# Attention inputs loaded tile by tile at separate points of the turn, row stores behind normalising, most zero stores later

## The chip, the cores and the metric

The kernel runs on one core of a Trainium2 chip. The metric is the device time of one execution in microseconds (us). TensorE has two clock levels, 1.2 and 2.4 GHz; the profile gives the granted clock as a share of the higher one.

## The reference: what is computed

Chunked local attention over q, k, v (8 batches, 8 heads, 576 positions, 64 wide, chunks of 64), then a noisy top-2 mixture of eight experts over the 4608 resulting rows of 512:

```python
scores = scale * np.matmul(q_c, k_c.transpose(0, 1, 2, 4, 3))
scores = scores - np.max(scores, axis=-1, keepdims=True)
attn = np.exp(scores)
attn = attn / (np.sum(attn, axis=-1, keepdims=True) + 1e-09)
out = np.matmul(attn, v_c)
...
noisy_logits = logits + noise_scale * noise
top2 = np.argpartition(-noisy_logits, 2, axis=1)[:, :2]
...
h = np.maximum(x[mask] @ w1[e], 0.0)
out[mask] += top2_w[mask, k, None] * (h @ w2[e])
```

## The kernel before, in words

**Tiling.** The 4608 rows are 36 tiles of 128. Attention runs in turns: `attend(it)` (line 679) is called with `it` from 0 to 35 (line 721), once more after that loop, and four more times from a hook inside the first expert block. A turn works on several tiles at once: scores of tile `it` on TensorE, their maximum and difference on VectorE and their exponential on ScalarE, the transpose of the probabilities of tile `it-1`, the product with v (`pv`) and the normalising (`norm_a`, `norm_b`, `norm_c`) of tile `it-2`, and the transpose of the finished rows (`x_trans`) of tile `it-3`. Every fourth turn adds the gate's matrix products, and `step_route` feeds in the routing of groups of tiles piece by piece.

**Order.** The schedule is written out by hand: each engine runs its instructions in the order of the code, and SP, which issues the plain DMAs, does so too. A DMA that must wait for an engine holds up all DMAs that stand behind it in SP's order. q, k and v are loaded by pairs of tiles: `load_q`, `load_k` (512 KB each) and `load_v` (520 KB). The loads of a pair stand at the start of every second turn and those of v at the end of every second turn. A tile's finished rows go to the buffer `xbuf` in HBM from within `x_trans` (line 464), one turn after `norm_c` wrote them.

**Around it.** The first expert's weights are loaded during attention: four loads of w1 in turns 12, 15, 18 and 21 (512 KB each), and four of w2 in turns 29, 31, 33 and 35. The output must be zeroed before experts add to it: 37 stores of 256 KB, of which `zero_out(1)` puts one into each turn from 20 to 35, and `hook_tail` (line 740) the other 21 into the first expert block (`layer1(0)`). `route` builds lists of rows; with them GpSimd gathers the rows of an expert block from `xbuf` (line 240), and later adds the results into the output (line 272). After attention the expert blocks follow one another on TensorE (`three`, line 305).

Of the kernel before, what the change touches and what calls it, by code (L numbers as in the profile page):

```python
# [8 lines left out]
FT = mybir.dt.float32  # L9
# [10 lines left out]
P = 128  # L20
NTOK = 4608
NT = NTOK // P
# [38 lines left out]
def kernel(ctx, tc, qT, kT, vh, wgn, noise, w1, w2, out, caps=CAPS):  # L61
    nc = tc.nc
# [4 lines left out]
    xbuf = dram.tile([NROWS, DM], FT, name="xbuf")  # L67
# [33 lines left out]
    for c in sorted(set(caps[1:])):  # L101
        n = caps.index(c, 1)
# [11 lines left out]
    stage = ctx.enter_context(tc.tile_pool(name="stage", bufs=4))  # L114
    W = {}
    staged = {}
# [3 lines left out]
    def w_load(e, which, c):  # L120
        st = stage.tile([P, 1024], FT, name="st")
        staged[e, which, c] = st
        if which == 1:
            nc.sync.dma_start(st, w1v[ds(place[e], 1), c].rearrange("o j r f -> (o j) r f") if e else w1[e, c * P:(c + 1) * P, :])
        else:
            nc.sync.dma_start(st.rearrange("p (f n) -> p f n", f=2),
                              w2[ds(place[e], 1) if e else slice(0, 1), 2 * c * P:(2 * c + 2) * P, :]
                              .rearrange("o (f p) n -> p (o f) n", f=2))
# [11 lines left out]
    PS = ctx.enter_context(tc.tile_pool(name="psum", bufs=1, space=PSUM)).tile([P, 8, 512], FT, name="PS")  # L140
# [221 lines left out]

    pa = ExitStack()
    pk = ExitStack()
    vs = pa.enter_context(tc.tile_pool(name="vs", bufs=4, side="right"))
    work = pa.enter_context(tc.tile_pool(name="work", bufs=3, side="right"))
    gx = pa.enter_context(tc.tile_pool(name="gx", bufs=2, side="right"))
    loads = pk.enter_context(tc.tile_pool(name="loads", bufs=4))
    qp, kb, vb = {}, {}, {}

    def load_q(j):
        qp[j] = loads.tile([P, 2, 4, P], FT, name="qp")
        if j:
            nc.sync.dma_start(qp[j], qT[:, 2 * j:2 * j + 2])

    def load_k(j):
        kb[j] = loads.tile([P, 2, 4, P], FT, name="kb")
        if j:
            nc.sync.dma_start(kb[j], kT[:, 2 * j:2 * j + 2])
        else:  # L380
            for t in range(2):
                nc.sync.dma_start(qp[0][:, t], qT[:, t])
                nc.sync.dma_start(kb[0][:, t], kT[:, t])

    def load_v(j):
        vb[j] = vs.tile([P, 2, 2, 4, 65], FT, name="vb")
        nc.sync.dma_start(vb[j], vh[:, 2 * j:2 * j + 2])

    nc.scalar.preload_act_table_set("natural_log_exp_and_others")
    for j in range(2):  # L390
        load_q(j)
        load_k(j)
    load_v(0)
    load_q(2)
    load_k(2)
    load_v(1)
    wg = consts.tile([P, ND, 32], FT, name="wg")
    nc.sync.dma_start(wg, wgn)
    nz = consts.tile([P, NT, NE], FT, name="nz")
# [1 line left out]

    zero = consts.tile([P, DM], FT, name="zero")
    nc.gpsimd.memset(zero, 0.0)
    nc.sync.dma_start(xbuf[0:P, :], zero)
    load_v(2)

    PR, PT, XS, XT, RC = {}, {}, {}, {}, {}

# [2 lines left out]
    HC = [(h, c) for h in range(2) for c in range(2)]  # L411

    def scores(t):
        q, k = qp[t // 2], kb[t // 2]
        for hp in range(4):
            for h, c in HC:
                r, s = slice(h * 64, h * 64 + 64), slice(c * 64, c * 64 + 64)
                o = 256 * (t % 2) + 64 * hp
                nc.tensor.matmul(PS[s, h, o:o + 64], q[r, t % 2, hp, s], k[r, t % 2, hp, s], start=True, stop=True)

    def soft_max(t):
        mx = work.tile([P, 2, 4], FT, name="mx", bufs=2)
        nc.vector.tensor_reduce(mx, sco(t), AX.X, OP.max)
        return mx

    def soft_sub(t, mx):
        PR[t] = work.tile([P, 512], FT, name="pr", bufs=2)
        nc.vector.tensor_tensor(by_head(PR[t]), sco(t), mx[:, :, :, None].to_broadcast([P, 2, 4, 64]), OP.subtract)
# [4 lines left out]
    def p_trans(t):  # L433
        for hp in range(4):
            nc.tensor.transpose(PS[:, 2, hp * P:(hp + 1) * P], PR[t][:, hp * P:(hp + 1) * P], ident)
        PT[t] = work.tile([P, 4, P], FT, name="pts", bufs=2)
        nc.scalar.activation(PT[t].rearrange("p a b -> p (a b)"), PS[:, 2, :], AF.Copy)
# [1 line left out]
    pvb = PS[:, 3:5, 0:260].rearrange("p b (g n) -> p b g n", n=65)  # L439

    def pv(t):
        v = vb[t // 2]
        for hp in range(4):
            for h, c in HC:
                r, s = slice(h * 64, h * 64 + 64), slice(c * 64, c * 64 + 64)
                nc.tensor.matmul(PS[s, 3 + h, hp * 65:hp * 65 + 65], PT[t][r, hp, s], v[r, t % 2, c, hp, :],  # L446
                                 start=True, stop=True)

    def norm_a(t):
        RC[t] = work.tile([P, 2, 4, 1], FT, name="rc", bufs=2)  # L450
        nc.scalar.activation(RC[t], pvb[:, :, :, 64:65], AF.Identity, bias=eps)

    def norm_b(t):
        nc.vector.reciprocal(RC[t], RC[t])

    def norm_c(t):
        XS[t] = work.tile([P, DM], FT, name="xs", bufs=5)
        nc.vector.tensor_tensor(by_head(XS[t]), pvb[:, :, :, 0:64], RC[t].to_broadcast([P, 2, 4, 64]), OP.mult)  # L458

    def x_trans(t):  # L460
        g, r = divmod(t, 4)
        if r == 0:
            XT[g] = gx.tile([P, ND, 4, P], FT, name="xt", bufs=1)
        nc.sync.dma_start(xbuf[(t + 1) * P:(t + 2) * P, :], XS[t])
        for d in range(ND):
            nc.tensor.transpose(PS[:, 5, d * P:(d + 1) * P], XS[t][:, d * P:(d + 1) * P], ident)  # L466
        nc.scalar.activation(XT[g][:, :, r, :], PS[:, 5, :].rearrange("p (d n) -> p d n", d=ND), AF.Copy)
# [3 lines left out]
    def gate_mm(g):  # L471
        for d in range(ND):
            nc.tensor.matmul(PS[32 * d:32 * d + 32, 6, :], wg[:, d, :], XT[g][:, d], start=True, stop=True)  # L473
        LS[g] = gx.tile([P, 4, P], FT, name="ls", bufs=1)
        nc.scalar.activation(LS[g].rearrange("p a b -> p (a b)"), PS[:, 6, :], AF.Copy)
# [3 lines left out]
    def gate_sum(g):  # L479
        q = grp_of[4 * g]  # L480
        t0, n = groups[q]
        if 4 * g == t0:
            Z[q] = gate.tile([P, n, 2, NE], FT, name=f"gz{q % 2}")
        for r in range(4):
            nc.tensor.matmul(PS[:, 6, 16 * r:16 * r + 16], LS[g][:, r, :], sel, start=True, stop=True)  # L485
        nc.scalar.activation(Z[q][:, 4 * g - t0:4 * g - t0 + 4].rearrange("p g a e -> p (g a e)"), PS[:, 6, 0:64], AF.Copy)
# [167 lines left out]
    def step_route(n):  # L654
        for _ in range(n):
            while routing:
                try:
                    next(routing[0])
                    break
                except StopIteration:  # L660
                    routing.pop(0)
# [11 lines left out]
    def zero_out(n):  # L673
        for _ in range(n):
            if zeros:
                r = zeros.pop(0)
                nc.sync.dma_start(out[r * P:(r + 1) * P, :], zero)

    def attend(it):
        STEPS = 2 if it < 33 else 3  # L680
        if it % 2 == 0 and it >= 2 and it // 2 + 2 < NT // 2:
            load_q(it // 2 + 2)
            load_k(it // 2 + 2)
        if it in (12, 15, 18, 21):
            w_load(0, 1, (it - 12) // 3)
        if it < NT:
            scores(it)
        if 0 <= it - 2 < NT:
            pv(it - 2)
            norm_a(it - 2)  # L690
        if 0 <= it - 1 < NT:
            p_trans(it - 1)
        if 0 <= it - 3 < NT:
            x_trans(it - 3)
        if it - 5 >= 0 and (it - 5) % 4 == 3:
            gate_sum((it - 5) // 4)
            if grp_of[it - 5] != grp_of.get(it - 4):
                routing.append(route(grp_of[it - 5]))
        if it - 4 >= 0 and (it - 4) % 4 == 3:
            gate_mm((it - 4) // 4)  # L700
        if it < NT:
            mx = soft_max(it)
            step_route(STEPS)
            soft_sub(it, mx)
            soft_exp(it)
        if 0 <= it - 2 < NT:
            norm_b(it - 2)
            norm_c(it - 2)
            if 0 <= it - (NT - 3) < 3:
                x_tile(0, it - (NT - 3), at=(6, 6, 5)[it - (NT - 3)])  # L710
            step_route(4 * STEPS)
        if it % 2 == 1 and it >= 3 and (it - 3) // 2 + 3 < NT // 2:
            load_v((it - 3) // 2 + 3)
        if it in (18, 19, 21, 22, 24, 25, 27, 28):
            w_split(0, 1, *wq.pop(0), eng=nc.gpsimd)
        if 20 <= it < NT:
            zero_out(1)
        if it in (29, 31, 33, 35):
            w_load(0, 2, (it - 29) // 2)

    for it in range(NT):
        attend(it)
# [118 lines left out]
    with tc.If(n_over > 0):  # L841
# [44 lines left out]
        with tc.For_i(0, n_over) as i:  # L886
# [19 lines left out]
            for f in range(NF):  # L906
                hp_ = PS[:, 1 + f % 2, 0:P]
                for d in range(ND):
                    nc.tensor.matmul(hp_, wa[:, d, f * P:(f + 1) * P], xt[:, d, :],
                                     start=(d == 0), stop=(d == ND - 1))  # L910
# [43 lines left out]
```

## Time and profile before

| | us |
|---|---|
| median of three runs | 1015.32 (1014.34 to 1018.19) |
| the profiled execution, its own time | 1017.64 |
| its span, first to last instruction | 1015.7 |
| TensorE busy in the span | 963.1 |
| VectorE / ScalarE / GpSimd busy | 459.0 / 310.4 / 479.8 |

The profiled execution had a mean granted clock of 0.985. A turn is the time from one tile's first score product (line 419) to the next tile's. Each engine's idle time carries the name of what ended it; "issue" means that the engine waited for nothing that the profile shows. The DMA queue q1 carries what SP issues, q8 and q14 carry instructions for the engines, q0 what GpSimd issues.

### The profile page before, as it was taken

How to read it: one execution, taken by the hardware profiler on the slowest of the kernel's cores; microseconds unless marked ns; L12 is line 12 of the kernel's file. 1: busy time of each engine (PE TensorE's matmuls, PEld its weight loads, DVE VectorE, ACT ScalarE, POOL GpSimd, SP SyncE). 2: the span in 40 equal slices, each digit the busy share in tenths (PEclk: the TensorE clock that was granted, in tenths of full speed). 3: DMA queues.
4: the chain of work that ended last, by engine and by line, in shares of the span. 5: the costliest groups of instructions: out<-in, count | busy, mean ns of one | idle time of the engine just before them, and what ended most of it. 6: DMA issues, size and time to landing. Idle time of an engine off the chain costs nothing.

```text
span 1015.7 us, 18418 instructions
## 1 busy us (share of the span) xinstructions
PE 963.1 (95%) x7353; PEld 859.0 (85%) x7353; DVE 459.0 (45%) x1001; ACT 310.4 (31%) x689; POOL 479.8 (47%) x619
## 2 busy tenths in 40 slices
PE   5878889999999999999999999999999999999994
PEld 4666768898888889988998999899988998899983
DVE  5577865653534343435333533453345334434311
ACT  3567765321323132213221322132223222223100
POOL 1023725335677568356734674467346725611111
PEclk9899998999999999999999999999999999999998
DMA  9979966333431543244324342444344334411212
GB/s 347 336 242 369 329 245 238 63 106 60 128 62 43 130 132 65 41 119 134 66 42 111 115 91 50 100 124 93 62 108 124 63 69 100 129 26 26 32 24 41
DMA packets 52233, 121.53 MB, mean 120 GB/s; under 512 B 8320, under 2 KB 9216, under 8 KB 52144
## 3 DMA queue, kind: packets, MB, share of 16 engines
q1 hardware_dynamic: 31984, 81.64, 22.2%
q0 software_dynamic: 20160, 38.69, 20.6%
q8 instruction: 58, 0.95, 0.4%
q14 instruction: 31, 0.25, 0.1%
HBM read 81.56 MB, written 38.73 MB: 118 GB/s over the span
## 4 chain that ended last, share of the span: by engine, by line
PE 82%; DVE 1%; issue 0%; ACT 0%; POOL 0%
PE PS L305 79%; PE PS L334 1%; PE PS L599 1%; PE PS L288 0%; DVE xl L296 0%; ACT xh L295 0%; POOL gohp L607 0%; PE PS L466 0%; DVE o L343 0%; PE PS L222 0%; DVE gmi L527 0%; PE PS L446 0%; PE PS L473 0%; PE PS L485 0%; DVE xs L458 0%
## 5 line engine op out<-in xcount | busy, mean ns | idle before, releaser
L260 POOL DMA_INDIRECT xg<-xbuf,piece x257 | 261.1, 1016 | 78.8 <-issue 71.0
L305 PE MATMUL PS<-xh,w1h 128*128 128x384 f32 (+2 forms) x768 | 263.2, 343 | 0.1
L305 PE MATMUL PS<-xl,w1h 128*128 128x384 f32 (+2 forms) x768 | 260.8, 340 | 0.3 <-DVE xl L296 0.3
L305 PE MATMUL PS<-xh,w1l 128*128 128x384 f32 (+2 forms) x768 | 260.6, 339 | 0.0
L305 PE MATMUL PS<-w2h,hh 128*128 128x512 f32 x584 | 228.8, 392 | 0.3 <-issue 0.3
L305 PE MATMUL PS<-w2l,hh 128*128 128x512 f32 x584 | 227.7, 390 | 0.2 <-issue 0.2
L305 PE MATMUL PS<-w2h,hl 128*128 128x512 f32 x584 | 227.7, 390 | 0.0
L272 POOL DMA_INDIRECT out<-o,lid x73 | 117.0, 1602 | 230.4 <-DVE o L343 208.8
L324 DVE SCALAR_TENSOR_TENSOR hl<-PS,hh 128x384 fp32r<-128x384 f32 (+1 forms) x192 | 107.0, 559 | 227.5 <-ACT hh L323 163.9
L323 ACT ACTIVATE hh<-PS 128x384 fp32r<-128x384 f32 (+1 forms) x192 | 94.1, 491 | 364.1 <-PE PS L305 313.1
L305 PEld LDWEIGHTS PS<-xh,w1h 128*128 128x128 f32 x768 | 144.6, 188 | 3.5 <-issue 0.8
L305 PEld LDWEIGHTS PS<-xl,w1h 128*128 128x128 f32 x768 | 144.6, 188 | 2.3 <-DVE xl L296 0.5
L305 PEld LDWEIGHTS PS<-xh,w1l 128*128 128x128 f32 x768 | 144.5, 188 | 1.0
L343 DVE TENSOR_SCALAR o<-PS,lwt 128x512 f32<-128x512 f32 x73 | 54.5, 749 | 190.7 <-PE PS L305 153.1
L305 PEld LDWEIGHTS PS<-w2h,hh 128*128 128x128 f32 x584 | 109.2, 187 | 23.9 <-issue 1.6
L305 PEld LDWEIGHTS PS<-w2h,hl 128*128 128x128 f32 x584 | 109.2, 187 | 23.5
L305 PEld LDWEIGHTS PS<-w2l,hh 128*128 128x128 f32 x584 | 109.2, 187 | 23.2 <-issue 0.9
L607 POOL TENSOR_SCALAR gohp<-row_p,gpf 128x128 f32<-128x128 f32 x36 | 26.6, 782 | 111.3 <-DVE gpf L591 101.1
L295 ACT ACTIVATE xh<-y 128x512 fp32r<-128x512 f32 x67 | 41.2, 615 | 109.1 <-DVE y L292 77.7
L296 DVE TENSOR_TENSOR xl<-y,xh 128x512 fp32r<-128x512 f32 x67 | 45.1, 673 | 48.0 <-ACT xh L295 31.0
L292 DVE STREAM_TRANSPOSE y<-xg 128x512 f32<-128x512 f32 x67 | 45.6, 680 | 2.3 <-DMA xg<-xbuf,piece 2.3
L138 DVE TENSOR_TENSOR w2l<-st,w2h 128x512 fp32r<-128x512 f32 x64 | 44.9, 702 | 0.0
(139 smaller groups left out, 792.9 us busy)
## 6 DMA issues: line engine op xcount, KB each, us to landing
st<-in_w SPq DMA_DIRECT2D x64, 512.0 KB
out<-zero SPq DMA_DIRECT2D x37, 256.0 KB
vb<-in_vh SPq DMA_DIRECT2D x18, 520.0 KB
xbuf<-xs SPq DMA_DIRECT2D x36, 256.0 KB
qp<-in_qT SPq DMA_DIRECT2D x17, 512.0 KB
kb<-in_kT SPq DMA_DIRECT2D x17, 512.0 KB
xg<-xbuf,piece POOLq DMA_INDIRECT x257
out<-o,lid POOLq DMA_INDIRECT x73
```

Source lines behind the costliest of these rows:

```text
L138: (eng or nc.vector).tensor_sub(lo[:, s], st[:, s], hi[:, s].bitcast(FT))
L260: nc.gpsimd.indirect_dma_start(out=XG[e, j][:, t * P:(t + 1) * P], out_offset=None, in_=xpieces, in_offset=bass.IndirectOffsetOnAxis(ap=pi ...
L272: s = nc.gpsimd.indirect_dma_start(out=to, out_offset=bass.IndirectOffsetOnAxis(ap=rows, axis=0), in_=o, in_offset=None, compute_op=OP.add)
L292: nc.vector.transpose(y[:, 0:4 * r], x[:, 0:4 * r])
L295: nc.scalar.activation(oh, src, AF.Copy)
L296: nc.vector.tensor_sub(ol, src, oh.bitcast(FT))
L305: nc.tensor.matmul(p, a, b, start=first and n == 0, stop=last and n == 2)
L323: nc.scalar.activation(hh[:, 0:m], p, AF.Relu)
L324: nc.vector.scalar_tensor_tensor(hl[:, 0:m], p, 0.0, hh[:, 0:m].bitcast(FT), op0=OP.max, op1=OP.subtract)
L334: nc.tensor.matmul(p[32 * q:32 * q + 32, 0:P], HF[0][:, f, 32 * t:32 * t + 32], w[:, q * P:(q + 1) * P], start=(f == 0), stop=(f == NF - 1))
L343: nc.vector.tensor_scalar(o[0:r], p[0:r], weights_of(i, j)[0:r], None, op0=OP.mult)
L607: nc.gpsimd.tensor_scalar(ohp[:, 0], row_p, pf[:, 0, 0, r:r + 1], None, op0=OP.is_equal)
```

## The change

- q, k and v have one buffer per tile in place of one per pair. `load_q` and `load_k` of tile `it+4` stand behind `scores(it)`, and `load_v` of tile `it+4` behind `pv(it-2)`; each moves 256 KB (v 260 KB). There are four buffers for q and k (four pairs before), and six for v (four pairs before).
- Before the first turn, four tiles of q, k and v are loaded (before: three pairs).
- The store of a tile's rows to `xbuf` moves from `x_trans` into `norm_c`, one turn earlier in SP's order.
- The first expert's weights come in halves of 256 KB, one a turn: w1 in turns 11 to 18, w2 in turns 28 to 35.
- Of the 37 zero stores, six stay in the last three turns of attention (two a turn), and 31 go to `hook_tail`. The zero store to the head of `xbuf` moves from before the first turn to turn 8.

```diff
-    vs = pa.enter_context(tc.tile_pool(name="vs", bufs=4, side="right"))
+    vs = pa.enter_context(tc.tile_pool(name="vs", bufs=6, side="right"))
...
+    def load_q(t):
+        qp[t] = loads.tile([P, 4, P], FT, name="qp")
+        nc.sync.dma_start(qp[t], qT[:, t])
...
+    def load_v(t):
+        vb[t] = vs.tile([P, 2, 4, 65], FT, name="vb")
+        nc.sync.dma_start(vb[t], vh[:, t])
...
-    for j in range(2):
-        load_q(j)
-        load_k(j)
-    load_v(0)
-    load_q(2)
-    load_k(2)
-    load_v(1)
+    for t in range(4):
+        load_q(t)
+        load_k(t)
+        if t:
+            load_v(t - 1)
...
-    nc.sync.dma_start(xbuf[0:P, :], zero)
-    load_v(2)
+    load_v(3)
...
     def norm_c(t):
...
+        nc.sync.dma_start(xbuf[(t + 1) * P:(t + 2) * P, :], XS[t])
...
     def x_trans(t):
...
-        nc.sync.dma_start(xbuf[(t + 1) * P:(t + 2) * P, :], XS[t])
...
+    def half_load(which, n):
+        c, h = divmod(n, 2)
+        if h == 0:
+            staged[0, which, c] = stage.tile([P, 1024], FT, name="st")
+        src = w1[0, c * P:(c + 1) * P, h * 512:h * 512 + 512] if which == 1 else w2[0, n * P:(n + 1) * P, :]
+        nc.sync.dma_start(staged[0, which, c][:, h * 512:h * 512 + 512], src)
+
     def attend(it):
         STEPS = 2 if it < 33 else 3
-        if it % 2 == 0 and it >= 2 and it // 2 + 2 < NT // 2:
-            load_q(it // 2 + 2)
-            load_k(it // 2 + 2)
-        if it in (12, 15, 18, 21):
-            w_load(0, 1, (it - 12) // 3)
         if it < NT:
             scores(it)
+        if it + 4 < NT:
+            load_q(it + 4)
+            load_k(it + 4)
         if 0 <= it - 2 < NT:
             pv(it - 2)
+        if it + 4 < NT:
+            load_v(it + 4)
+        if 0 <= it - 2 < NT:
             norm_a(it - 2)
...
-        if it % 2 == 1 and it >= 3 and (it - 3) // 2 + 3 < NT // 2:
-            load_v((it - 3) // 2 + 3)
...
-        if 20 <= it < NT:
-            zero_out(1)
-        if it in (29, 31, 33, 35):
-            w_load(0, 2, (it - 29) // 2)
+        if 11 <= it < 19:
+            half_load(1, it - 11)
+        if NT - 8 <= it < NT:
+            half_load(2, it - NT + 8)
+        if it == 8:
+            nc.sync.dma_start(xbuf[0:P, :], zero)
+        if NT - 3 <= it < NT:
+            zero_out(2)
```

## Rows read from the trace of the kernel before

**Rows 1.** Busy time by stretch: length, PE, PEld, DVE, ACT, POOL, clock, DMA share, GB/s.
```profile
20.00:54.00 34.00, 26.70 (x631) 21.81 (x633) 18.33 (x35) 17.74 (x38) 0.00 (x0) 0.85 0.87 319
...
205.00:1015.70 810.70, 794.54 (x4255) 717.92 (x4253) 322.73 (x547) 194.68 (x407) 414.78 (x527) 0.99 0.35 82
```

**Rows 2.** Waits of PE in 17:54: total us, times, longest us.
```profile
PE PS L466 <- issue: 2.2, 1, 2.2
```

**Rows 3.** Timeline of PE: start us, us, instruction, idle before it.
```profile
17.59 1.02 PE L419 MATMUL PS<-kb,qp 64*64 64x64 f32 x31
...
20.18 0.69 PE L419 MATMUL PS<-kb,qp 64*64 64x64 f32 x32
...
24.43 0.37 PE L435 MATMUL PS<-ident,pr 128*128 128x128 f32 x1 [2.08 <-issue]
...
25.59 1.13 PE L419 MATMUL PS<-kb,qp 64*64 64x64 f32 x32
...
29.41 1.13 PE L419 MATMUL PS<-kb,qp 64*64 64x64 f32 x32
...
51.34 0.56 PE L446 MATMUL PS<-vb,pts 64*64 64x65 f32 x18 [1.33 <-issue]
```

**Rows 4.** Busy time by stretch again, columns as in Rows 1.
```profile
18.10:24.42 6.32, 3.93 (x127) 3.31 (x127) 4.28 (x8) 2.96 (x7) 0.00 (x0) 0.94 1.03 407
24.42:37.68 13.26, 12.13 (x254) 9.97 (x253) 6.55 (x12) 8.15 (x17) 0.00 (x0) 0.77 0.91 338
...
25.00:30.00 5.00, 5.00 (x96) 4.22 (x98) 2.18 (x4) 2.96 (x6) 0.00 (x0) 0.50 0.92 362
45.00:50.00 5.00, 5.00 (x126) 3.75 (x118) 2.33 (x5) 2.49 (x6) 0.00 (x0) 0.74 1.02 380
```

**Rows 5.** DMA queues (packets, MB, share) in 21.9:23.1, then 51.4:52.4, then 52.4:53.8.
```profile
q8 instruction: 1, 0.02, 5.5%
...
q1 hardware_dynamic: 11, 0.02, 6.3%
...
q8 instruction: 1, 0.02, 5.4%
```

**Rows 6.** Timeline of SP's queue, first issue and that at 23.96.
```profile
0.72 0.41 SPq L382 DMA_DIRECT2D qp<-in_qT  x1
...
23.96 5.51 SPq L464 DMA_DIRECT2D xbuf<-xs  x2
```

**Rows 7.** What the DMA engines moved in 0:24.4.
```profile
DMA packets 3022, 8.40 MB, mean 344 GB/s; under 512 B 327, under 2 KB 583, under 8 KB 3020
```

**Rows 8.** Waits of PE in 108:150.
```profile
PE PS L446 <- issue: 1.2, 3, 0.4
PE PS L466 <- issue: 1.1, 1, 1.1
```

**Rows 9.** Waits of PE in 0:17, and line 419's waiting instructions (ns).
```profile
PE PS L419 <- DMA kb<-in_kT: 7.2, 2, 4.2
...
L419 PEldq EVENT_SEMAPHORE  x19: 51/51/51, 4.1 to 138.5; - x19
```

**Rows 10.** DMA in 3:5 (loads of 2 KB packets), and SP's zero stores after attention.
```profile
DMA packets 291, 0.54 MB, mean 270 GB/s; under 512 B 27, under 2 KB 27, under 8 KB 291
...
159.50 14.31 SPq L677 DMA_DIRECT2D out<-zero  x21
```

**Rows 11.** Timelines of POOL and PE after attention.
```profile
181.48 1.05 POOL L240 DMA_INDIRECT xg<-xbuf,lid  x1 [4.38 <-DVE lid L211]
...
189.98 1.65 POOL L272 DMA_INDIRECT out<-o,lid  x1 [4.84 <-DVE run L552]
...
187.08 0.60 PE L288 MATMUL PS<-ident,xg 128*128 128x128 f32 x4
```

**Rows 12.** Timeline of PE: scores of tiles 11 and 19.
```profile
44.68 1.13 PE L419 MATMUL PS<-kb,qp 64*64 64x64 f32 x32
...
77.04 0.69 PE L419 MATMUL PS<-kb,qp 64*64 64x64 f32 x32
```

More of the change, by code (lines that the diff above doesn't have):

```diff
@@ L369, with load_k @@
     qp, kb, vb = {}, {}, {}
[L371 to L387, printed above, removed]
-    nc.scalar.preload_act_table_set("natural_log_exp_and_others")
-    for j in range(2):
-        load_q(j)
-        load_k(j)
-    load_v(0)
-    load_q(2)
-    load_k(2)
-    load_v(1)
+    def load_q(t):
+        qp[t] = loads.tile([P, 4, P], FT, name="qp")
+        nc.sync.dma_start(qp[t], qT[:, t])
+    def load_k(t):
+        kb[t] = loads.tile([P, 4, P], FT, name="kb")
+        nc.sync.dma_start(kb[t], kT[:, t])
+    def load_v(t):
+        vb[t] = vs.tile([P, 2, 4, 65], FT, name="vb")
+        nc.sync.dma_start(vb[t], vh[:, t])
+    nc.scalar.preload_act_table_set("natural_log_exp_and_others")
+    for t in range(4):
[3 more added lines that the diff above has]
+            load_v(t - 1)
     wg = consts.tile([P, ND, 32], FT, name="wg")
@@ L413, in scores @@
     def scores(t):
-        q, k = qp[t // 2], kb[t // 2]
+        q, k = qp[t], kb[t]
         for hp in range(4):
@@ L418, in scores @@
                 o = 256 * (t % 2) + 64 * hp
-                nc.tensor.matmul(PS[s, h, o:o + 64], q[r, t % 2, hp, s], k[r, t % 2, hp, s], start=True, stop=True)
+                nc.tensor.matmul(PS[s, h, o:o + 64], q[r, hp, s], k[r, hp, s], start=True, stop=True)
     def soft_max(t):
@@ L441, in pv @@
     def pv(t):
-        v = vb[t // 2]
+        v = vb[t]
         for hp in range(4):
@@ L445, in pv @@
                 r, s = slice(h * 64, h * 64 + 64), slice(c * 64, c * 64 + 64)
-                nc.tensor.matmul(PS[s, 3 + h, hp * 65:hp * 65 + 65], PT[t][r, hp, s], v[r, t % 2, c, hp, :],
+                nc.tensor.matmul(PS[s, 3 + h, hp * 65:hp * 65 + 65], PT[t][r, hp, s], v[r, c, hp, :],
                                  start=True, stop=True)
```

## The prediction

> **What bounds the kernel now.** I read the busy time by stretch first. After 205 us TensorE (PE) is busy 794.5 of 810.7 us [rows 1]: the expert blocks are bound by PE, and the change does not touch their work. So whatever attention gains or loses moves the end by as much. Between 20 and 54 us it is otherwise: PE is busy 26.7 of 34 us, and at a mean clock of 0.85 [rows 1]. Next I read PE's waits in that stretch, and what stands out are not the inputs. No wait for a load of q, k or v is among them; the long ones are "issue": 2.2 us [rows 2], 1.33 us, and 2.08 us in the middle of a group of four transposes, whose operands were all there [rows 3]. Their sum is 5.6 us.
>
> What does PE wait for in mid-group? The counts tell. From 18.10 us, where PE last paused, to 24.42, the end of the 2.08 us stall, PE and its weight loads ran 127 and 127 instructions; from there to the stall that ends at 37.68 they ran 254 and 253 [rows 4]. The pauses stand 254 or so instructions apart, or twice that. And inside each there is a packet of 0.02 MB on the instruction queue: one lies in 21.9 to 23.1 us, and PE goes on at 24.43 [rows 3, 5]. So PE is out of instructions, and waits for its next block.
>
> How late is a block? I take it that it is asked for when the block before it is begun. The one just named was then asked for at 18.10 and started at about 21.9: 3.8 us of waiting while SP's queue was full. Its transfer (5.5% of 16 engines over 1.2 us, 1.06 us) and the 1.4 us up to 24.43 make the rest of the 6.3 us. One with an idle queue shows the floor: after the 1.33 us stall, which ends at 51.34 [rows 3], the share of SP's queue is 6.3%, and the next block starts just behind 52.4 [rows 5], 1.1 us after it was asked for. A block then costs 1.1 + 1 + 1.4 = 3.5 us. A plain turn takes 2.59 us (17.59 to 20.18) [rows 3] and has 144 instructions by the code (32 + 32 + 4 + 4 products, each with its weight load), so 254 last 4.6 us. A block is hidden if it waits up to about 2 us; at 3.8 it is not. So this stretch is bound by instruction blocks that stand behind bursts of data.
>
> **The change part by part.** The profiled execution took 1017.64 us, 2.3 above the median of 1015.32; I sum against the profile and carry the difference over to the median.
>
> **Loads by tile, gated by the turn.** How full is the queue in either kernel? By 24.4 us SP had issued, from 0.72 to 23.96 [rows 6], 26 DMAs: four of 256 KB for the first pair, ten of 512 KB for q and k, five of 520 KB for v, four stores and one zero store of 256 KB, and 208 KB of gate and noise: 10.5 MB. Moved were 8.40 MB [rows 7]. So 2.1 MB stood in line. With the changed code and PE at the same point (scores of tile 5 and pv of tile 3 done, rows of tile 3 written) SP may have issued q, k and v of ten tiles, four stores and the 208 KB: 9.2 MB. That leaves 0.8 MB. As 2.1 MB mean a wait of some 3.8 us, 0.8 MB mean about 1.4 us: under the 2 us that a turn hides. It stays so if the DMAs keep up: four transfers a turn at 0.68 us each (21 zero stores in 14.31 us [rows 10]) are 2.7 us, against the 3.1 us that a turn takes on average here once the gate's products are in it (estimate: 2.6 us, and about 1 us more in every second turn).
>
> What there is to win: the 5.6 us of stalls, and the slow clock behind them. After the 2.1 us stall the granted clock is 0.50 (1.2 GHz) from 25 to 30 us, and after the 2.2 us one it is 0.74 on average from 45 to 50 [rows 4]. The turn from 25.59 to 29.41 takes 3.82 us in place of 2.59 [rows 3], so 1.2 us lost; in 45 to 50 about half the time is slow, so some 0.65. Together 7.45 us. I take 80%, since the queue starts full and the first block may still come late: **-6.0** (bounds 0 and -7.5).
>
> The same loss is there later: PE's "issue" waits in 108 to 150 us are 1.2 and 1.1 us [rows 8], while a zero store stood in every turn. Without it 2.3 us can go; 80% is **-1.8** (bounds 0 and -2.3).
>
> **Start.** PE waited 7.2 us for k in two waits [rows 9], 4.2 for the first tile, which the change leaves alone, and 3.0 for the second, whose two transfers are the third and fourth in either order. What stands behind them is smaller. I take **-0.5** (bounds -3.0 and +1.3, the latter if a packet lags again).
>
> **More waits.** Line 419 has 19 waiting instructions of 51 ns [rows 9]; single tiles want some 18 more, and v's may want as many: **+0.9** (bounds 0 and +1.8). What is queued behind them is PE's own turn. On SP each load now waits for PE (q and k for the scores that free their buffer, v for pv), and behind it wait that turn's store, its half of weights and the next loads. Nobody needs them within three turns (7.8 us at 2.6), so that costs nothing as long as a load lands within that time.
>
> **Row stores and weights.** The store waits for `norm_c` of its own turn where it waited for the last turn's; readers are gathers many turns later. The w1 halves come in turns 11 to 18, and their first splitting is in turn 18, so nothing waits. Nothing for these.
>
> **Zero stores.** Ten more go behind attention: 10 x 0.68 = 6.8 us of queue [rows 10]. Cover: the first addition into the output is issued at 189.98, waiting for VectorE, not for zeros [rows 11]; 31 stores from 159.5 would end at about 180.6. PE there runs long products, and a block of instructions lasts far longer. The gathers issued from 181.48 are needed at 187.08 [rows 11]; with attention shorter by 7 us both move, and the last zeros with them. Six zeros and w2's halves crowd turns 33 to 35: a block could come late once: **+0.5** (bounds 0 and +2).
>
> Sum: -6.0 - 1.8 - 0.5 + 0.9 + 0.5 = -6.9, thus 1010.7 for an execution like the profiled one, and **1008.4** beside the median.
>
> The DMA page of the Trainium skill ("DMA: Bandwidth & Descriptors", section "Rules for kernel authors") speaks against small transfers: full bandwidth wants at least 1 MiB in each DMA. In the row above 256 KB stores run back to back at 385 GB/s, which does not bear it out; by the page alone the loads would get slower, and the sum would be that of the second rival.
>
> **Rivals.** *The blocks don't hang on the queue (no change).* The block's request can't be seen; if blocks start late by a rule of their own, and not because they stand behind data, the stalls stay, and only start, waits and the end count: -0.5 + 0.9 + 0.5 = +0.9, so 1016. For it: I inferred the request. Against it: with an idle queue the block started 1.1 us after the stall's end, with a full one 3.8 us. I give it 0.25. The Trainium skill ("Runtime: NRT & Kernel Launch", section "Instruction fetch mechanics") has a rule of that kind: blocks of 16 KiB (256 instructions) are fetched ahead of time and crossing into the next is mostly hidden, and PE's memory holds 2048 of them; by it there would be no such stall to win back. The trace agrees with 256 and 16 KiB, and not with "hidden".
>
> *Loads by 2 KB pieces are slow (slower).* From 3 to 5 us only loads of 256 KB ran, at 270 GB/s [rows 10], which is 0.97 us each. If that held throughout, turns 11 to 18 would need 3 x 0.97 + 0.68 + 0.97 for the half of weights = 4.56 us of DMA; they take (77.04 - 44.68)/8 = 4.05 now [rows 12]. 0.5 x 8 = 4.1 us, the stalls stay as the queue stays full, and the last three turns with six zeros add some 3, waits 0.9: +8, so 1023. It decides where a load takes over 0.84 us (4 x 0.84 + 0.68 = 4.05). Against it: those 2 us are the start, when the engines were not all busy yet. I give it 0.08.
>
> *Half.* Blocks get earlier, but the first three stalls of the start stay, as the queue is full from the initial loads whatever the order: about -3, so 1012. I give it 0.07.
>
> **How the numbers follow.** Forecast 0.60, with a range of its own from 1002 (all bounds good) to 1012. 0.5% is 5.1 us, about what a measurement of this kernel can tell from no change. Of the forecast's 0.60, 0.55 lie below 1010.2 and 0.05 above. So faster 0.55; same 0.05 + 0.25 + 0.07 = 0.37; slower 0.08. The range of 8 in 10 is 1002 to 1016.5: below lie 0.04, above the slow rival and some of the no-change case, together about 0.15.
>
> **What would show it.** Right: PE's "issue" waits before 54 us under 2 us in sum where 5.6 stand now; clock near 1.00 from 25 to 30 and from 45 to 50; the scores of tile 19, at 77.04 now [rows 12], at about 70.5; no wait of PE for loads after tile 3; the 31 zero stores done before the first addition into the output. Wrong: stalls that stay 254 instructions apart with the same lengths though the queue is emptier; waits of line 419 for k or q; turns of over 4 us at 11 to 18 with a DMA share of 1.

## The result, and the profile after

The changed kernel takes 1010.02 us in the median (1008.16 to 1010.53), the kernel before, run beside it, 1017.53 us (1014.34 to 1018.56). The ratio is 0.9917, with a 95% interval of 0.9896 to 0.9938: about 7.5 us faster, where -6.9 was forecast. The two profiled executions, 1017.64 and 1010.38 us, are 7.3 us apart, and their spans, 1015.7 and 1008.6 us, 7.1 us.

Busy time by stretch of the kernel after (columns as in [rows 1]):

```profile
20.00:54.00 34.00, 25.26 (x686) 20.36 (x685) 22.37 (x68) 20.50 (x46) 0.00 (x0) 1.00 1.01 371
54.00:150.00 96.00, 79.72 (x1778) 66.08 (x1778) 72.07 (x244) 65.94 (x167) 39.66 (x51) 0.95 0.81 274
205.00:1008.60 803.60, 786.76 (x4217) 710.39 (x4215) 319.32 (x541) 191.21 (x400) 412.43 (x524) 1.00 0.35 81
```

The first line answers to the first of [rows 1]. In the same 34 us PE ran 686 products where it had run 631, in less busy time, as the clock was 1.00 and no longer 0.85. The DMA engines did not get any emptier: their share went from 0.87 to 1.01, and 319 GB/s became 371. The second line holds something that nothing had forecast: the clock is 0.95 there. In the profile of before on which the prediction rests it is 1.00, and in another profile of before, taken later, 0.95 too (the same stretch in these two):

```profile
54.00:150.00 96.00, 78.30 (x1887) 64.32 (x1879) 73.72 (x244) 68.84 (x175) 39.80 (x51) 1.00 0.88 312
54.00:150.00 96.00, 81.01 (x1853) 66.86 (x1849) 73.01 (x243) 67.73 (x172) 39.60 (x51) 0.95 0.87 306
```

So a slow clock there is not shown to come from the change. The last line of the three has nearly the work of before (4217 products against 4255, the window is not cut at the same instruction), so the expert blocks are as they were.

PE's waits between 17 and 54 us, all of them "issue" that the view lists (columns as in [rows 2]):

```profile
PE PS L426 <- issue: 2.4, 1, 2.4
...
PE PS L437 <- issue: 1.5, 2, 0.8
...
PE PS L457 <- issue: 0.6, 1, 0.6
```

That is 4.5 us. The same view of before has 6.0 us (the 5.6 us of the three large ones and 0.4 us). So PE still runs out of instructions. The long pause stands in turn 5 as it did before [rows 3], again in the middle of a group of four transposes (PE's timeline, columns as in [rows 3]):

```profile
18.06 0.69 PE L410 MATMUL PS<-kb,qp 64*64 64x64 f32 x32
...
19.45 0.44 PE L426 MATMUL PS<-ident,pr 128*128 128x128 f32 x2
22.31 0.38 PE L426 MATMUL PS<-ident,pr 128*128 128x128 f32 x2 [2.43 <-issue]
...
23.06 0.69 PE L410 MATMUL PS<-kb,qp 64*64 64x64 f32 x32
23.57 0.65 PE L437 MATMUL PS<-vb,pts 64*64 64x65 f32 x32
...
25.46 0.69 PE L410 MATMUL PS<-kb,qp 64*64 64x64 f32 x32
```

The difference is in what follows. The turn behind the pause takes 2.40 us (23.06 to 25.46), where before it took 3.82 us [rows 3] at a clock of 0.50 [rows 4].

Where did the gain arise? The starts of the score products, tile by tile, give a ledger (us, from PE's timelines). The first two columns are the profiles spoken of so far; "again" is a second profile of each kernel, from executions of 1014.99 and 1014.33 us, reported below:

| start of | before | after | gain so far | before, again | after, again | gain so far |
|---|---|---|---|---|---|---|
| tile 1 | 8.34 | 7.16 | 1.2 | 7.25 | 7.06 | 0.2 |
| tile 5 | 20.18 | 18.06 | 2.1 | 19.58 | 17.64 | 1.9 |
| tile 13 | 53.65 | 46.37 | 7.3 | 53.62 | 47.58 | 6.0 |
| tile 23 | 92.70 | 85.37 | 7.3 | 92.66 | 86.59 | 6.1 |
| tile 24 | 98.47 | 92.03 | 6.4 | 99.93 | 93.44 | 6.5 |
| tile 26 | 105.06 | 98.63 | 6.4 | 106.52 | 100.03 | 6.5 |
| tile 27 | 108.88 | 103.90 | 5.0 | 111.82 | 105.38 | 6.4 |
| tile 29 | 117.40 | 112.40 | 5.0 | 120.32 | 113.87 | 6.5 |
| tile 30 | 121.91 | 115.60 | 6.3 | 123.52 | 117.08 | 6.4 |
| tile 35 | 144.41 | 138.13 | 6.3 | 145.98 | 141.63 | 4.4 |
| first expert block | 151.84 | 145.55 | 6.3 | 153.41 | 149.06 | 4.4 |
| end of the span | 1015.7 | 1008.6 | 7.1 | 1013.2 | 1012.4 | 0.8 |

Before tile 13 already 7.3 us are won, and 6.0 us in the second pair: this part is in both. In the first pair the turns of tiles 23 and 26 give back 0.9 and 1.5 us, and the turn of tile 29 wins 1.3 us; in the second pair none of the three is there, but the turn of tile 31 gives back 2.1 us. The last 0.8 us of the first pair lie behind the start of the expert block, and I did not trace them to a line. In the second pair 3.6 us are lost there, and the products of line 334, spoken of below, take 4.1 us longer in that profile of after.

The two turns of after that give back in the first pair run at a slow clock (busy time by stretch, columns as in [rows 1]):

```profile
84.00:88.00 4.00, 2.34 (x67) 2.11 (x68) 3.88 (x28) 1.42 (x3) 1.27 (x1) 0.76 0.74 255
88.00:92.00 4.00, 2.73 (x24) 1.57 (x22) 2.48 (x8) 2.01 (x5) 0.00 (x0) 0.81 0.71 245
100.00:104.00 4.00, 4.00 (x43) 3.71 (x39) 3.87 (x7) 3.65 (x11) 4.00 (x6) 0.61 0.93 311
```

and the first of them starts behind a pause that has nothing to do with DMAs. PE waits there for VectorE's softmax (PE's timeline):

```profile
85.37 0.69 PE L410 MATMUL PS<-kb,qp 64*64 64x64 f32 x32 [2.18 <-DVE pr L419]
86.35 1.15 PE L437 MATMUL PS<-vb,pts 64*64 64x65 f32 x32 [0.29 <-DVE gm L514]
```

At full clock 32 products of line 437 take 0.65 us (at 23.57 above), here 1.15. Before has the same pause in the same place:

```profile
92.70 0.69 PE L419 MATMUL PS<-kb,qp 64*64 64x64 f32 x32 [2.22 <-DVE pr L428]
```

In this profile its clock stays at 1.00 behind the pause (92 to 96 us), and the turns of tiles 23 and 26 take 5.77 and 3.82 us. In the second profile of before they take 7.27 and 5.30 us, as slow as in after (6.66 and 5.27).

### The profile page after: what moved, and what is told of

Read it like the earlier page. It is cut to its first block, busy times and chain, and to the rows that moved or that the text cites. A ratio compares the mean times of both kernels' runs of the same rounds, so it can differ in the third digit from the quotient of the medians.

```text
span 1008.6 us, 18542 instructions
## 1 busy us (share of the span) xinstructions
PE 959.2 (95%) x7353; PEld 856.3 (85%) x7353; DVE 458.0 (45%) x1001; ACT 309.6 (31%) x689; POOL 479.6 (48%) x619
## 4 chain that ended last, share of the span: by engine, by line
PE 82%; DVE 1%; issue 1%; ACT 0%; another core or an unknown queue 0%; POOL 0%; DVEq 0%; ACTq 0%
PE PS L305 79%; PE PS L334 1%; PE PS L590 1%; ACT xh L295 0%; PE PS L288 0%; DVE xl L296 0%; POOL gohp L598 0%; PE PS L457 0%; DVE o L343 0%; PE PS L222 0%; ACT hh L323 0%; DVE gmi L518 0%; PE PS L437 0%; PE PS L464 0%
```

## Experiments

The prediction's theory was: the loads are the source (**A** in the texts on record), because they are released turn by turn and so fewer bytes stand ahead of an instruction block. Against it stood that the blocks have a rule of their own and do not hang on the data. The profile after raised two more questions, as the DMA engines were as full as before and the time was still won: is it the **size** of the transfers (**C**) or the **point** at which they are released (**D**)? A ratio below is to the kernel before, beside it on the same chip, with its 95% interval. The median of before was between 1010.9 and 1017.6 us in these comparisons, so ratios are to be compared, not times.

### One part alone

**Only the loads tile by tile**, in the kernel before; row stores, weights and zeros stay.

```diff
+    def load_q(t):
+        qp[t] = loads.tile([P, 4, P], FT, name="qp")
+        nc.sync.dma_start(qp[t], qT[:, t])
...
+        if it + 4 < NT:
+            load_q(it + 4)
+            load_k(it + 4)
```

> The kernel before with the tile-by-tile loads alone; weights, row stores and zero stores stay where they were. Theory A (the loads in small pieces, gated by the turn, let PE's instruction blocks come earlier and spare the slow clock): most of the gain is here, -5 to -7 us, with tile 13's scores near 46.5 us (53.65 before, 46.37 with the whole change) and the later stall of 1.1 us near turn 30 still there. Rival B (the gain comes from the zero stores and weights that were moved): within 1.5 us of before.

Measured: 0.9948 (0.9927 to 0.9969), 1011.20 us against 1017.63 us, so 5 us or so of the whole gain. From the scores of tile 5 to those of tile 13 its profile has 27.19 us, against 33.47 in before and 28.31 in after. The loads carry most of the gain. Tile 13 starts at 45.59 us, even before the 46.5 that was expected; the later stall near turn 30 is not there, though the zero stores stand where they stood (the turn of tile 29 takes 3.20 us, and 4.51 in before).

**Only the zero stores later**, in the kernel before.

```diff
-        if 20 <= it < NT:
-            zero_out(1)
+        if it == 8:
+            nc.sync.dma_start(xbuf[0:P, :], zero)
+        if NT - 3 <= it < NT:
+            zero_out(2)
```

> The kernel before with the zero stores alone moved. The first 75 us are then as before. Theory A: only the later block waits go (2.3 us before, 1.3 of it regained at turn 30 with the whole change), so -1 to -2 us. Rival B: -5 or more.

Measured: 0.9988 (0.9965 to 1.0011). If it brings anything, it is about 1 us, which these runs do not tell from nothing. Tile 13 starts at 50.98 us in its profile (53.65 and 53.62 in the two of before), where no change was expected before 75 us.

**All but the loads.** The changed kernel, with q, k and v loaded by whole pairs at the old places.

```diff
-        if it + 4 < NT:
-            load_q(it + 4)
-            load_k(it + 4)
...
+        if it % 2 == 0 and it >= 2 and it // 2 + 2 < NT // 2:
+            load_q(it // 2 + 2)
+            load_k(it // 2 + 2)
```

> The changed kernel with q, k and v loaded as before (whole pairs of 512 and 520 KB at their old places); weights in halves, row stores, zero stores and the head's zero store are the changed ones. Theory C (the size of the loads makes most of the gain): -0.5 to -2.5 us against before. Rival (the parts overlap, and the rest would give the gain alone too): -5 or more.

Measured: 0.9987 (0.9966 to 1.0007). Row stores, weights in halves and zero stores together are worth some 1.3 us if anything, which is not told from nothing.

### Size or place

**Only the size.** The kernel before, each transfer of a pair issued as two of 256 KB, at the old places and into the old buffers.

```diff
-            nc.sync.dma_start(qp[j], qT[:, 2 * j:2 * j + 2])
+            for t in range(2):
+                nc.sync.dma_start(qp[j][:, t], qT[:, 2 * j + t])
```

> The kernel before with each load of a pair issued as two DMAs of half the size at the same place in SP's order; buffers and gates are those of pairs. Theory C (what counts is how many bytes SP can have outstanding; smaller DMAs bound it): more than half of the gain of the small loads, -3 to -5 us, the blocks' waits before 54 us under 4 us. Theory D (what counts is that loads are released by the turn they follow): no change, within 1.5 us.

Measured: 0.9943 (0.9917 to 0.9970). This is as much as the loads tile by tile gave, without any new place. PE's "issue" waits in 17 to 54 us of its profile are still 4.9 us, more than was expected, and tile 5 to 13 takes 31.98 us; the profiled execution (1013.46 us) is above this kernel's median of 1012.15 us.

**The size without the place, with all the rest.** The changed kernel, loads by pairs at the old places, each as two of 256 KB. It differs from "all but the loads" above in the size alone, and from the changed kernel in place and buffers of the loads alone.

```diff
-        if it + 4 < NT:
-            load_q(it + 4)
-            load_k(it + 4)
...
+            for t in range(2):
+                nc.sync.dma_start(qp[j][:, t], qT[:, 2 * j + t])
```

> The changed kernel, but q, k and v are loaded by pairs of tiles at the places of the kernel before, each pair as two DMAs of 256 KB. Theory C (smaller DMAs are what helps; where they are released does not matter): within 1.5 us of the changed kernel, so -6.5 to -9. Theory D (release by tile at separate points helps by itself): at least 2 us slower than the changed kernel, so -6 or less.

Measured: 0.9948 (0.9929 to 0.9967); the changed kernel once more, on the same chip:

> The changed kernel once more, for a second profile and for times beside the runs below. Expected: -7 to -9 us. If the stalls before 54 us and the spells of slow clock are set by the program they stand at the same turns as in the first profile (stall in turn 5 of about 2.4 us, slow clock in turns 23 and 26); if they are chance they stand elsewhere while the time is the same.

gave 0.9936 (0.9913 to 0.9959). The two are not told apart: the place brings nothing that these runs can show. The size does: 0.9948 against 0.9987, each to before on its own chip. Their profiles say where: tile 5 starts at 18.44 us with halves and 19.81 us with whole pairs (1.4 us); tile 5 to 13 takes 26.69 against 28.76 us (2.1 us); tile 13 to 35 takes 90.82 against 93.22 us (2.4 us). That is 5.8 of the 5.9 us between the spans (1007.9 and 1013.8 us). But 1.7 of the last 2.4 us are the turn of tile 23 (5.23 against 6.89 us), which differs by 1.5 us between the two profiles of before as well.

The second profile of the changed kernel answers what was asked of it: the pause stands in turn 5 again (2.0 us), and the turns of tiles 23 and 26 are slow again (6.85 and 5.35 us). "Issue" is 5.9 us in 17 to 54 us, where the first profile had 4.5 us, and tile 5 to 13 takes 29.94 us, against 28.31.

How does the size act? SP's issues in before, and then in after (start us, us, line, operation, out<-in):

```profile
9.65 0.33 SPq L404 DMA_DIRECT2D xbuf<-zero  x1
10.88 0.33 SPq L387 DMA_DIRECT2D vb<-in_vh  x1
12.15 0.33 SPq L374 DMA_DIRECT2D qp<-in_qT  x1
```

```profile
8.65 0.33 SPq L381 DMA_DIRECT2D vb<-in_vh  x1
9.58 0.33 SPq L373 DMA_DIRECT2D qp<-in_qT  x1
10.22 0.33 SPq L377 DMA_DIRECT2D kb<-in_kT  x1
10.89 0.33 SPq L381 DMA_DIRECT2D vb<-in_vh  x1
```

SP needs 0.33 us for an issue but issues only every 1.27 us with 512 KB, and every 0.65 us with 256 KB: either way some 400 KB per us, the rate of the DMA engines. It waits for landings (SP's waits in before; that of line 374 is the issue at 12.15 above, that of line 379 the next one, at 13.42):

```profile
SPq L374 <- DMA vb<-in_vh: 0.9, 1, 0.9
SPq L379 <- DMA qp<-in_qT: 0.9, 1, 0.9
```

The records of SP's DMAs in the traces say for which landings: the DMAs carry eight semaphores in turn, and each waits for the DMA that carried its semaphore before it, eight issues earlier. In before the issue at 12.15 starts 0.02 us behind the landing of the v load issued at 3.56, and in after that at 10.22 starts 0.02 us behind the landing of the v load issued at 4.03. So no more than eight transfers are under way, whatever their size; it is this program that sets the eight, and the place of a load in the code does not alter it. The bytes in line then go with the size. Issued less moved, the mean of ten instants from 9 to 23 us, is 1.8 to 2.2 MB in the four profiles with 512 KB (before twice, only the zeros, all but the loads), and 1.2 to 1.3 MB in the five with 256 KB (after twice, only the loads, only the size, pairs halved).

So it is at the end of the pause of turn 5 in after (DMAs from 0 to 22.3 us):

```profile
DMA packets 4015, 7.07 MB, mean 317 GB/s; under 512 B 440, under 2 KB 696, under 8 KB 4013
...
qp<-in_qT SPq DMA_DIRECT2D x10, 256.0 KB
vb<-in_vh SPq DMA_DIRECT2D x9, 260.0 KB
kb<-in_kT SPq DMA_DIRECT2D x9, 256.0 KB
xbuf<-xs SPq DMA_DIRECT2D x3, 256.0 KB
nz<-in_noise SPq DMA_DIRECT2D x1, 144.0 KB
wg<-in_wgn SPq DMA_DIRECT2D x1, 64.0 KB
```

Issued are 31 transfers of 256 or 260 KB and 208 KB: 8.4 MB. Moved are 7.07 MB, so 1.3 MB are in line, as much as the last five transfers. Before it was 2.1 MB [rows 6, 7], which is the last five transfers too: two stores of 256 KB, and v, q and k of 520 and 512 KB. The next block, by the prediction's rule asked for when PE goes on at 22.31, lies in 25 to 26 us (queue q8 there):

```profile
q8 instruction: 1, 0.02, 5.5%
```

It starts at about 25.1 us: 2.8 us of waiting, against 3.8 us. By the same rule, and with 127 products to a block, the next five blocks up to 54 us waited 2.5 to 2.9 us; those of before waited 3.7 to 4.6 us, up to the one that met an idle queue. In the second profiles it is 1.6 to 4.0 us (3.0 in the mean) for after and 3.6 to 4.4 us (4.0) for before. One block of the first profile of after does not fit, that of the long pause itself. Counted back by 127 products it was asked for at 15.8 us, and it lies in 19.2 to 20.2 us (queue q8 there):

```profile
q8 instruction: 1, 0.02, 6.7%
```

It starts at 19.95 us: 4.1 us of waiting, as long as before, behind some 1.2 MB. This is why the pause of turn 5 did not get shorter; why this block came so late is open.

Do fewer bytes in line mean less waiting of PE? "Issue" in 17 to 54 us is 6.0, 8.3, 5.9 and 3.3 us in the four profiles with 512 KB, and 4.5, 5.9, 3.4, 4.9 and 2.6 us in the five with 256 KB. The mean is smaller, 4.3 in place of 5.9 us, but the two overlap. That the size acts through the blocks fits the waits of the blocks, and is not shown beyond that; that it makes the kernel faster is shown by the times.

### Do the blocks hang on the data at all?

**No loads after the first six tiles.** The kernel before; later tiles take the q, k and v of the first six again, so that only the time is read, and of it the stretch before 54 us.

```diff
+        if j > 2:
+            qp[j] = qp[j - 3]
+            return
```

> The kernel before, but q, k and v are loaded for the first six tiles only, and later tiles compute with these again; the output is then not the reference's, and routing and all that follows differ. Only the first 54 us are read. Theory (PE's instruction blocks wait behind data in the queue): from about 20 us on the blocks arrive 3.5 us after they are asked for, no issue wait of PE above 0.3 us, clock 1.00, and tile 13's scores some 25 us after tile 5's (33.5 before). Rival (blocks come late by a rule of their own): PE still pauses every 254 or 508 instructions for 1 to 2 us.

Measured: 1005.17 us. Between 17 and 54 us "issue" does not occur among PE's waits, which now wait for the softmax (first PE's waits there, then 20 to 54 us by busy time):

```profile
PE PS L444 <- ACT pr L440: 2.8, 5, 0.9
PE PS L428 <- DVE pr L437: 2.0, 2, 1.3
```

```profile
20.00:54.00 34.00, 28.18 (x800) 23.08 (x792) 25.98 (x78) 22.46 (x53) 0.00 (x0) 1.00 0.34 119
```

With a DMA share of 0.34 tile 5 to 13 takes 24.27 us, which is the pace of the engines. The same instructions in the same order no longer run out. So the blocks wait behind data, and the rival with a rule of their own falls. The Trainium skill ("Runtime: NRT & Kernel Launch", section "Instruction fetch mechanics") says that crossing into the next block is mostly hidden. This run agrees with that, and the traces of before and after, at a DMA share of 0.87 and 1.01, do not.

**Smaller still.** The changed kernel, each load as two transfers of 128 KB, one for each half of the partitions.

```diff
-        nc.sync.dma_start(qp[t], qT[:, t])
+        for r in (slice(0, 64), slice(64, P)):
+            nc.sync.dma_start(qp[t][r], qT[r, t])
```

> The changed kernel with each load of q, k and v as two DMAs of 128 KB (64 partitions each, the same 2 KB rows). Theory C (PE's blocks wait behind what SP has outstanding, eight DMAs at a time): the bytes ahead of a block fall by up to half, blocks wait under 2 us, the issue waits before 54 us fall from 4.5 to under 2 us, and the time falls by 1 to 3 us below the changed kernel (-9 to -11 in all). Rival: SP's issuing (seven DMAs a turn at 0.4 us = 2.8 us) becomes the bound of the 2.4 us turns, loads land late, and the time is 1 to 4 us above the changed kernel.

Measured: 1.0348 (1.0320 to 1.0376), 1053.12 us. Far worse, and beyond what was expected even of the worse case. SP's issues, and then PE's only wait listed in 17 to 54 us:

```profile
21.58 1.18 SPq L374 DMA_DIRECT2D qp<-in_qT  x2
22.80 1.23 SPq L379 DMA_DIRECT2D kb<-in_kT  x2
24.08 1.69 SPq L384 DMA_DIRECT2D vb<-in_vh  x2
```

```profile
PE PS L413 <- DMA kb<-in_kT: 10.7, 10, 2.1
```

```profile
20.00:54.00 34.00, 23.20 (x521) 19.59 (x520) 15.29 (x28) 13.74 (x31) 0.00 (x0) 0.85 0.71 216
```

Issue follows issue with hardly a gap, and each takes some 0.6 us, the row store's too (0.66 us in this stretch), where it was 0.33 us in the changed kernel. Six of them are 3.6 us a turn before the store, so SP itself sets the pace. Whether the half partitions or the number of transfers lengthen an issue was not tried apart. The DMA engines are no longer full (0.71), PE waits for k, and no "issue" is left. This does not speak for or against blocks that wait behind data: PE ran only 521 products in this stretch, where after had 686, so each block lasted longer and could wait longer unseen.

### Fewer bytes in line by other means

**Three tiles ahead in place of four.**

```diff
-        if it + 4 < NT:
-            load_q(it + 4)
-            load_k(it + 4)
+        if it + 3 < NT:
+            load_q(it + 3)
+            load_k(it + 3)
```

> The changed kernel with loads three tiles ahead in place of four. Theory C: 0.8 MB less in line at the start, the stall of turn 5 gets shorter by 1 us or more, so 0.5 to 2 us below the changed kernel. Rival: three turns are too short a lead while the queue is full; line 410 waits for q or k after tile 3, and the time is 1 us or more above the changed kernel.

Measured: 0.9940 (0.9913 to 0.9966), not told from the changed kernel. In the profile the turn of tile 5 takes 3.80 us in place of 5.00, and tile 5 to 13 26.96 us.

**Row stores held back.** The changed kernel with ten buffers for finished rows, whose stores start in turn 9.

```diff
-        XS[t] = work.tile([P, DM], FT, name="xs", bufs=5)
+        XS[t] = work.tile([P, DM], FT, name="xs", bufs=10)
...
+            save_rows(0 if it < 9 else 1 if it < 20 else 2)
```

> The changed kernel with the row stores held back: none until turn 9, then one a turn, two a turn from turn 20 (ten buffers for the rows in place of five). It takes a quarter of the DMA traffic out of turns 2 to 8. Theory C (blocks wait behind data while the DMAs are saturated): DMA share under 1 from about turn 7 on, issue waits before 54 us under 2 us, tile 13's scores at 44 to 45 us, 1.5 to 3 us below the changed kernel. Rival (what is left of the early loss is the start, when the queue is full whatever is stored): within 1 us of the changed kernel.

Measured: 0.9925 (0.9897 to 0.9953). "Issue" is 3.6 us before 54 us, where under 2 us was expected; tile 13 starts at 44.97 us. Again not told from the changed kernel.

**The kernel before, another profile,** for how much one profile says.

> The kernel before once more, for a second profile. If the first profile was typical, the pauses for instruction blocks before 54 us sum to 5 to 6 us again and spells of slow clock follow the two longest; the wait for the second tile's k (3.0 us) is chance if it is near 1.7 us here, as in the four variants with small or other loads behind it.

Measured: 1014.99 us. "Issue" before 54 us is 8.3 us here, against 6.0 us in the profile on which the prediction rests. Tile 1 starts at 7.25 us, not at 8.34. Tile 5 to 13 takes 34.04 us (33.47). After the pauses the clock is 1.00 from 25 to 30 us, not 0.50, and the spells of slow clock lie elsewhere: the turn of tile 26 takes 5.30 us as it does in after, where the first profile had 3.82 us. And the turn of tile 29 takes 3.20 us, not 4.51: the late pause of 1.1 us is missing here. So the stalls before 54 us are the kernel's; how long they are in sum, and where the clock falls, is the execution's.

**Both together:** three tiles ahead, and row stores held back.

> The changed kernel with both steps that left least in the queue early on: loads three tiles ahead, and row stores held back until turn 9. Theory C: DMA share under 0.95 from 20 to 54 us, issue waits of PE before 54 us under 2.5 us (4.5 in the changed kernel), 1 to 3 us below the changed kernel, so -8 to -11 us against before. Rival (each variant's difference from the changed kernel was chance, and slow clock later gives back what is won early): -6 to -8 us, as the changed kernel.

Measured: 0.9883 (0.9859 to 0.9907), 998.63 us against 1010.86 us. It beats both kernels, and by more than was expected. The profiled execution, 1002.33 us, is the slowest of the six. PE's waits in 17 to 54 us that are "issue" come to

```profile
PE PS L438 <- issue: 0.9, 2, 0.6
```

and the stretch is

```profile
20.00:54.00 34.00, 27.58 (x759) 22.45 (x757) 25.16 (x76) 21.53 (x50) 0.00 (x0) 0.99 0.95 313
```

The blocks come nearly in time, and tile 5 to 13 takes 25.28 us, 1 us above the pace without loads. But by the start of the expert block only 1.0 us of that is left (144.57 against 145.55 us in after), as a slow spell in the turn of tile 15 (clock 0.75, 1.7 us) and a pause of 1.0 us on "issue" in the turn of tile 18 take it back. So this kernel, too, still has such a pause, only later. Most of the 8.1 us between this span and that of after (1000.5 and 1008.6 us) arises later. From the first of 128 small products of line 334 to the next group are 3.6 us here and 8.9 us in after (PE's timeline, this kernel and then after):

```profile
314.21 3.70 PE L334 MATMUL PS<-st,hf 128*32 128x128 f32 x128
```

```profile
...
319.13 0.46 PE L334 MATMUL PS<-st,hf 128*32 128x128 f32 x5 [0.32 <-issue]
319.89 0.43 PE L334 MATMUL PS<-st,hf 128*32 128x128 f32 x4 [0.31 <-issue]
...
324.34 1.32 PE L334 MATMUL PS<-st,hf 128*32 128x128 f32 x37 [1.02 <-issue]
```

That is 5.2 us in a place that no edit touches. The DMA engines are nearly idle there in both (a share of 0.14 in after, 0.16 here). Why this execution is spared I cannot say. The other profiles vary in the same place: 8.9 and 5.3 us in the two of before, 7.9 and 9.5 us with either edit alone.

## Why the prediction was right, and which steps were not

**The bound was read rightly.** Between 20 and 54 us PE is held up by instruction blocks behind bursts of data: without loads there is no such pause. The end moves by what attention gains in the first pair of profiles, 6.3 us at the start of the expert block and 7.1 us at the end. It does so only within what the expert blocks vary by themselves: in the second pair 4.4 us became 0.8 us.

**Loads, -6.0; the size was right, the way was not.** From tile 5 to tile 13 5.2 us are gained. The step that failed is "that leaves 0.8 MB", with blocks that wait 1.4 us. I took it that release by turn keeps the queue nearly empty. It does not: SP runs ahead until its buffers or its eight semaphores stop it, the share rose to 1.01, and 1.3 MB stood in line. The sum had set 9.2 MB issued against the 8.40 MB that before had moved by 24.4 us; PE got there 2.1 us earlier, when 8.4 MB were issued and 7.07 MB moved. The blocks waited 2.5 to 2.9 us, and that of turn 5 4.1 us. "Issue" therefore fell by 1.5 us only in this pair of profiles (2.4 us in the second), not by 80% of 5.6. What made up for it in this pair is the clock: the slow spells in the turns of tiles 6 and 11 are gone (3.82 to 2.40 us, and 4.41 to 3.29 us). And the cause inside the loads is not the point of release, on which my argument stood, but the size of a transfer: halves at the old places gain as much. Of the signs that I named, "issue" under 2 us before 54 us did not appear; those of the clock (1.00 from 25 to 30 and from 45 to 50 us) and of tile 19 (69.71 us, 70.5 said) did, and no load was waited for after tile 3. The clock came true partly by the luck of the execution: in the second profile of before the turns of tiles 6 and 11 take 2.41 and 3.29 us already.

**Start, -0.5:** it was -2.1 at tile 5, inside the bounds, near the good one of -3.0. 1.2 us of it are there at tile 1, and of these most are an outlier of the first profile of before, since its other one starts tile 1 at 7.25 us. The rest grows from tile 1 to tile 5; both profiles of after have it (10.90 and 10.58 us for these four tiles, against 11.84 and 12.33 us).

**Later pauses, -1.8:** one is gone in the first pair of profiles, the 1.14 us one in the turn of tile 29 (1.3 us). But the second profile of before does not have it, nor does that with only the loads changed, where a zero store still stands in every turn. So it was the execution's, and the term rested on one profile. The small ones remain: "issue" in 54 to 150 us is 2.7 and 1.4 us in the two profiles of before, and 1.5 and 1.9 us in those of after. Nobody forecast the 2.35 us that the slow clock gives back in the turns of tiles 23 and 26. They, too, are a difference of executions, as the second profile of before is slow there as well.

**More waits, +0.9:** line 410 has 36 waiting instructions where line 419 had 19, and PE has 14 more in all: 0.7 us at 51 ns each, at most.

**End, +0.5:** nothing. The last three turns take 14.06 us from tile 32 to tile 35, and 14.07 before. The cover named for the zeros held (SP, and then GpSimd, of after):

```profile
153.23 21.35 SPq L668 DMA_DIRECT2D out<-zero  x31
```

```profile
175.20 1.05 POOL L240 DMA_INDIRECT xg<-xbuf,lid  x1 [4.38 <-DMA out<-zero]
...
183.71 1.65 POOL L272 DMA_INDIRECT out<-o,lid  x1 [4.84 <-DVE run L543]
```

The zeros are issued until 174.6 us. The first addition, at 183.71, waits for VectorE. The view puts the gathers' wait of 4.38 us down to a zero store, but it was as long before [rows 11], and what they need comes last, as it did there: VectorE writes their list of rows (line 211) from 174.75 to 174.92 us, and they start at 175.20. That is 6.3 us earlier than before, as attention ends 6.3 us earlier.

**The rivals.** Blocks with a rule of their own: fell with the run without loads. Slow 2 KB loads: fell, as 371 GB/s were moved in 20 to 54 us. The Trainium skill ("DMA: Bandwidth & Descriptors", section "Rules for kernel authors") wants at least 1 MiB in a DMA for full bandwidth. Here 256 KB beat 512 KB. The 128 KB over 64 partitions agree with its direction, at 42 us more than the changed kernel's 1011.26 us on the same chip, but what held that kernel was SP's issuing, with a DMA share of 0.71.

So the forecast was near the time partly by luck. Block waits won less than was said, start and clock more, and of these the clock, the later pause and the two turns that gave some back are differences between executions. What both pairs show is the gain of 6.0 to 7.3 us up to tile 13.

## What to carry to other kernels

Where an engine idles on "issue" at even counts of instructions while the DMA share is near 1, ask whether it is out of instructions; a run without the loads told it here. What counts then is the bytes ahead of its next block. Where SP's transfers wait for one another, as they do here eight issues apart, their size sets these bytes, so make the large loads smaller while SP can still issue them faster than they move. Hold back what nobody needs yet: fewer tiles ahead and later stores together took nearly all of the pauses before 54 us away here, each alone did not. Take two profiles of each kernel before you put a gain down to a turn, and read it from totals as well: a stage's time in one profile can move by more than the change under study.

## What the runs showed that I had not expected

- With each load halved over the partitions SP's issues took some 0.6 us each, back to back, where they had taken 0.33 us; the kernel became 42 us slower.
- What bounds SP's queue here is eight semaphores that the program's DMAs share, not the place in the code: 1.27 us between issues of 512 KB, 0.65 us between those of 256 KB, with 2.1 and 1.3 MB in line.
- The clock fell to 0.50 behind a pause in one profile of before and stayed at 1.00 behind as long a pause in the other. Which pauses are followed by a slow spell (2.35 us lost here, 1.2 us there) is open.
- 128 dense small products of line 334 take 3.6 us at best and up to 10.1 us (in the profile with pairs halved and all the rest), in pieces of four to six with 0.31 us of "issue" between. What they wait for is not shown: the DMA engines are nearly idle there, and in after a single instruction block comes in these 9 us, at 320.1. Why one profile escaped it is open, and with it some 5 of the 12 us that the last experiment gained.
